# Column norms from squares, query weights turned by DMA, and a written order of decisions in a two-layer linear-attention kernel

## The chip, the cores and the metric

The kernel runs on one core of a Trainium2 chip. A core has a matrix engine (TensorE, PE in the profile), three engines for vectors (VectorE or DVE, ScalarE or ACT, GpSimd or POOL), an engine that issues transfers (SyncE, SP) and 16 DMA engines. Each engine works through its own list of instructions in order, and engines wait for each other on semaphores. The metric is the device time of one execution in microseconds, as a median over runs.

## The reference

There are 2048 tokens of 576 numbers, and two rounds of two blocks, each added to its input. Block A is linear attention with 32 heads of 18 numbers; its features are two softmaxes, of a small projection and of its negative. Block B multiplies two wide projections (4608 columns) and projects back. Both rounds use the same weights.

```python
qkv = (x @ wqkv) ...                       # q, k, v: 32 heads of 18
pq = einsum("bhsd,hdf->bhsf", q, w_phi)    # the same for pk from k
phi_q = concatenate([softmax(pq), softmax(-pq)])
kv = einsum("bhsf,bhsd->bhfd", phi_k, v);  z = sum of phi_k over tokens
o = (phi_q @ kv) / (phi_q . z + 1e-6);     A = o.reshape(B, S, D) @ wo
B = ((x @ w_gate) * (x @ w_up)) @ w_down
x = x + A(layernorm(x)); x = x + B(layernorm(x))     # twice
```

## The kernel before, in words

Tokens are cut into 16 tiles of 128 and, for block B, into 8 blocks of two tiles. The 576 channels are cut into four pieces of 128 and one of 64. The small matrix w_phi is folded into the query and key weights first: t_fuse1 (L1112) turns each of five 128-row pieces of the raw weights Wraw around (L1125, five matmuls with an identity into PSUM, and a copy at L1128 into WTk or WTq), multiplies by the block-diagonal BDphi (L1139) and evicts the two halves into Wk or Wq (L1144). A branch for turning them by DMA (L1120) is in the code and is not taken, since the string wtdma is empty.

Softmax needs no maximum when the logits are bounded. A flag decides this at run time. t_m2 (L971) finds the largest absolute entry of w_phi, and t_flag (L989) bounds the column norms of the query and key weights. For each of the five pieces it multiplies ten 128-column slices of Wraw by themselves into two PSUM banks (L999); the diagonals of these Gram matrices hold the squared norms, and a maximum over each row (L1002) is at least as large. A comparison (L1008), two matmuls with a vector of ones (L1010) that count the rows within the bound, and a last comparison (L1012) make the flag. Each engine then waits for the flag, loads it into a register and branches (emit_two, L221): one program without maxima ("fast") and one with them. What was recorded ahead of the flag is common to both; everything else lies behind the branch.

Stage one of layer 1 takes each tile through LayerNorm (t_ln, L1155; statistics L1179, normalised rows L1212, then turned by TensorE at L1223 for the first four tiles and by DMA at L1230 for the others), the V projection (t_v, L1463, eviction L1488) and the key projection (fast_front, L1363, exponentials L1377). softmax_tail (L1430) sums the features (L1444), inverts the sums, on DVE (L1447) or ACT (L1451, L1455), and multiplies (L1459, on POOL or DVE). Keys and values of a pair of tiles are then accumulated into two PSUM banks (L1498, t_ain). Query projections (t_qproj, L1387, copies at L1401 on ACT or L1402 on DVE) need nothing of that sum and can run at any time once Wq is there and the key tile given by pqg is done. After all 16 tiles t_barrier masks the sums, t_aout (L1598) forms the attention output of a tile, and block B starts on tiles 0 and 1 while later tiles follow in between: gate and up products (L1788), their product (L1835, L1837), and the down product (L1862, L1864). K, V and query projections run in pairs on the lower and upper 64 rows of the array (L1256, called row matmuls here); transposes, fusion and accumulation use the full array.

The order on every engine is fixed ahead of time by a planner in the kernel file (Sched, L316). Each piece of work is a thread that asks for an instruction or a group; the planner keeps an estimate of when each engine is free and takes the thread whose group could start first, moved forward or back by a priority, by an age from the code, and by an age from the table AGES (L19). Where a group is offered on two engines ("alt") it takes the one that ends first by its estimates. Engines keep the order in which their groups were taken. SP has one list as well: the loads of raw weights, tokens and V weights in the order of sload (L708), the transposing DMAs, the weights of block B.

## Time and profile before

| | |
|---|---|
| median of 5 runs | 1062.31 us |
| lowest and highest run | 1059.61 and 1062.66 us |
| profiled execution, its own time | 1061.52 us |
| its span, first to last instruction | 1059.7 us |
| mean granted TensorE clock | 0.998 |
| TensorE busy | 1052.1 us |
| VectorE, ScalarE, GpSimd busy | 480.3, 346.8, 190.7 us |
| DMA traffic | 127.78 MB |

A line of the timeline gives the start, the length, the engine, the line of the kernel, the operation, its output and inputs with their sizes, and in brackets how long the engine was idle before and what released it. In the answers by window the columns are the busy times of PE, PEld (the loading of matmul weights), DVE, ACT and POOL with their instruction counts, the granted clock, the DMA share and the traffic. Matmul ends are modelled, so the distance from one start to the next says what a matmul costs. A list of waits gives the total, the count and the longest.

### The profile page before, as it was taken

Reading aid. Unit: us, or ns where it says so; the run is one execution under the profiler, and the core shown is the slowest. Engines: PE = TensorE matmul, PEld = TensorE weight load, DVE = VectorE, ACT = ScalarE, POOL = GpSimd, SP = SyncE. Lnnn points to the kernel's source line nnn. Section 1 sums busy time; section 2 is a strip of 40 time slices with the busy share of each in tenths; the row PEclk is TensorE's granted clock in tenths of the full one; section 3 lists DMA queues with packets and bytes.
Section 4 is the critical chain, followed back from the end, with each engine's and each line's share of the span. In section 5 each row is a group of like instructions: output and inputs, shape, how many; then the busy total and the mean of one; then the engine's idle time right before and its main releaser. Section 6 shows DMA issues by size and latency. Waiting matters only on the chain.

```text
span 1059.7 us, 34388 instructions
## 1 busy us (share of the span) xinstructions
PE 1052.1 (99%) x15851; PEld 804.5 (76%) x15851; DVE 480.3 (45%) x972; ACT 346.8 (33%) x843; POOL 190.7 (18%) x204
## 2 busy tenths in 40 slices
PE   8999999999999999999999999999999999999998
PEld 6777868687786868778696786877778686868685
DVE  7865545264444536444232663534334343424131
ACT  6876224133241413225141742222313131202020
POOL 3962113030221203003110020201010101000000
PEclk9999999999999999999999999999999999999999
DMA  4595282552808165351616034545271918181704
GB/s 157 108 340 167 37 229 47 163 101 72 179 15 225 39 180 84 86 143 37 202 15 199 5 60 139 124 103 160 70 193 37 225 15 237 26 225 16 211 4 149
DMA packets 177625, 127.78 MB, mean 121 GB/s; under 512 B 96576, under 2 KB 175680, under 8 KB 176320
## 3 DMA queue, kind: packets, MB, share of 16 engines
q1 hardware_dynamic: 176864, 125.47, 45.5%
q8 instruction: 126, 2.06, 0.8%
q14 instruction: 27, 0.22, 0.1%
q10 hardware_dynamic: 608, 0.02, 0.0%
HBM read 100.82 MB, written 2.36 MB: 97 GB/s over the span
## 4 chain that ended last, share of the span: by engine, by line
PE 95%; DMA 2%; POOL 1%; ACT 1%; DVE 1%; issue 0%
PE ps L1788 54%; PE ps L1862 22%; PE ps L1256 12%; PE ps L1864 3%; PE ps L1646 1%; DMA wdr<-in_B_w_down_dram 1%; PE ps L1498 1%; PE ps L1244 0%; PE ps L1223 0%; POOL dd_w3f L1459 0%; POOL dd_h1g L1459 0%; DMA wdx<-in_B_w_down_dram 0%; ACT dd_h1g L1377 0%; DMA wst<-in_A_w_phi_dram 0%; POOL xln L1212 0%; PE ps L1139 0%
## 5 line engine op out<-in xcount | busy, mean ns | idle before, releaser
L1788 PE MATMUL ps<-xT,Wu 64*128 64x256 bf16 x4608 | 581.6, 269 | 0.0
L1788 PE MATMUL ps<-xT,Wg 64*128 64x256 bf16 x4608 | 581.1, 269 | 0.0
L1788 PEld LDWEIGHTS ps<-xT,Wg 64*128 64x128 bf16 x4608 | 431.2, 94 | 30.6 <-issue 3.3
L1788 PEld LDWEIGHTS ps<-xT,Wu 64*128 64x128 bf16 x4608 | 432.3, 94 | 27.6
L1837 DVE TENSOR_TENSOR hT<-ps,hT 128x512 bf16<-128x512 f32 x288 | 199.1, 691 | 302.5 <-ACT hT L1835 302.5
L1835 ACT CAST hT<-ps 128x512 bf16<-128x512 f32 x288 | 168.5, 585 | 400.5 <-PE ps L1788 396.2
L1862 PE MATMUL ps<-wdr,hT 128*128 128x512 bf16 x960 | 245.4, 380 | 0.4 <-DMA wdr<-in_B_w_down_dram 0.3
L1459 POOL TENSOR_TENSOR dd<-dd,ss 128x576 bf16<-128x576 bf16 x92 | 106.6, 1184 | 441.6 <-ACT ss L1455 441.6
L1864 PE MATMUL ps<-wdr,hT 128*128 128x64 bf16 x960 | 185.0, 193 | 0.0
L1862 PEld LDWEIGHTS ps<-wdr,hT 128*128 128x128 bf16 x960 | 93.7, 98 | 111.1 <-DMA wdr<-in_B_w_down_dram 1.8
L1788 PE MATMUL ps<-xT,Wr 64*128 64x256 bf16 x1152 | 165.5, 269 | 0.0
L1212 POOL TENSOR_SCALAR xln<-x_sb,nmean,rstd 128x576 bf16<-128x576 bf16 x56 | 45.5, 822 | 332.5 <-DVE nmean L1193 151.2
L1905 DVE TENSOR_TENSOR x_sb<-ps,x_sb 128x64 bf16<-128x64 f32 x32 | 7.0, 220 | 213.4 <-PE ps L1864 213.4
L1864 PEld LDWEIGHTS ps<-wdr,hT 128*128 128x128 bf16 x960 | 94.4, 98 | 0.2
L1455 ACT ACTIVATE ss<-ss 128x64 f32<-128x64 f32 x92 | 23.8, 259 | 195.9 <-DVE ss L1444 195.1
L1444 DVE TENSOR_REDUCE ss<-dd 128x64 f32<-128x1152 bf16 x48 | 63.7, 1345 | 16.6 <-ACT dd L1377 10.8
L1788 PEld LDWEIGHTS ps<-xT,Wr 64*128 64x128 bf16 x1152 | 63.2, 94 | 6.5
L1862 PE MATMUL ps<-wdx,hT 128*128 128x512 bf16 x192 | 54.4, 380 | 0.3 <-DMA wdx<-in_B_w_down_dram 0.3
L1256 PE MATMUL ps<-Wv,xT 64*128 64x288 bf16 x576 | 50.4, 288 | 0.2 <-ACT dd_h1g L1377 0.2
L1256 PE MATMUL ps<-Wk,xT 64*128 64x288 bf16 x576 | 48.4, 283 | 0.1
L1179 DVE BATCH_NORM_STATS2 st<-x_sb 128x6 f32<-128x288 bf16 x120 | 46.2, 445 | 0.8 <-DVE flag L1012 0.7
L1256 PE MATMUL ps<-Wq,xT 64*128 64x288 bf16 x576 | 40.6, 283 | 0.0
(131 smaller groups left out, 739.7 us busy)
## 6 DMA issues: line engine op xcount, KB each, us to landing
wdr<-in_B_w_down_dram SPq DMA_DIRECT2D x240, 288.0 KB, 3.6
wdx<-in_B_w_down_dram SPq DMA_DIRECT2D x48, 288.0 KB, 3.7
Wg<-in_B_w_gate_dram SPq DMA_DIRECT2D x4, 1152.0 KB, 17.1
Wu<-in_B_w_up_dram SPq DMA_DIRECT2D x4, 1152.0 KB, 18.5
out_dram<-x_sb SPq DMA_DIRECT2D x16, 144.0 KB, 2.5
x_sb<-in_A_x_dram SPq DMA_DIRECT2D x7, 288.0 KB, 3.2
Wraw<-in_A_wqkv_dram SPq DMA_DIRECT2D x5, 304.0 KB, 4.4
xT<-xln SPq DMA_TRANSPOSE x54, 2.5
```

Source lines behind the costliest of these rows:

```text
L1179: ops.append(Op(d_dve(288), (lambda e, j=j, h=h, src=src: e.bn_stats(st[:, sl[j], 6 * h:6 * h + 6], src)), reads=rd, writes=[("st", sl[j], ...
L1212: em = (lambda e, j=j: e.tensor_scalar(xln[:, sl[j], 0:576], x_sb[:, ss[j], :], s.nmean[:, sl[j]:sl[j] + 1], rstd[:, sl[j]:sl[j] + 1], ALU ...
L1256: out.append(Op(61, (lambda e, h=h, k=k, st=(i == 0 and k == 0), sp=(i == 1 and k == 3): e.matmul(s.ps[:, banks[h], 0:N], L[r, k, :], Wm[r ...
L1444: Op(1265, (lambda e: e.tensor_reduce(ss[:, sm, :], e4, AX.X, ALU.add)), reads=s.ddk(sm, 0) + s.ddk(sm, 1), writes=[("ss", sm)]),
L1455: yield ("ops", "act", [Op(200, (lambda e, kw=kw: e.activation(ss[:, sm, :], ss[:, sm, :], **kw)), reads=[("ss", sm)], writes=[("ss", sm)])])
L1459: yield ("alt", [(eng, [Op(dur, (lambda e, ev=ev, rb=rb: e.tensor_tensor(ev, ev, rb, ALU.mult)), reads=s.ddk(sm, br) + [("ss", sm)], write ...
L1498: ops.append(Op(d_pe(CW * n) + 3, (lambda e, k=k, c0=c0, h=h, n=n, st=(first and k == bi): e.matmul(s.ps[:, bank, c0:c0 + CW * n], phi[:, ...
L1788: out.append(Op(54.3, (lambda e, bank=bank, cs=cs, lhsT=lhsT, rhs=rhs, st=st, sp=sp: e.matmul(ps[:, bank, cs].rearrange("p (a n) -> p a n" ...
L1835: yield ("ops", "act", [Op(480, (lambda e, gb=gb, p=p: e.copy(hT[:, p, :], ps[:, gb, :])), reads=[("gu", gb)], writes=[("hT", p)] + (s.raw ...
L1837: yield ("ops", "dve", [Op(600, (lambda e, ub=ub, p=p: e.tensor_tensor(hT[:, p, :], ps[:, ub, :], hT[:, p, :], ALU.mult)), reads=[("gu", u ...
L1862: ops = [Op(d_pe(512), (lambda e: e.matmul(s.ps[:, bank, 0:512], lhsT, s.wslot(slot)[:, fi, 0:512], start=(f == 0), stop=(f == NF - 1))), ...
L1864: Op(d_pe(64) + 3, (lambda e: e.matmul(s.ps[:, z, 64 * sl:64 * sl + 64], lhsT, s.wslot(slot)[:, fi, 512:576], start=(f == 0 and (sl == 0 o ...
```

## The change

There are four edits. The flag's norms are no longer taken from Gram matrices: each piece of Wraw is squared (on ACT, or on POOL), nine matmuls per piece with a column of ones add the squares over rows into nine PSUM columns, and one maximum over nine columns follows; one comparison and one matmul take the place of two columns and two matmuls, and the limit is lowered by 1/64. The query weights are turned by the DMA branch of t_fuse1. Key and value accumulations are grouped by a list kvg, whose value gives the same pairs as before. And a text ORDER lists, decision by decision, which thread is to be taken next and in some places on which engine; as long as words are left, the planner takes the waiting thread whose next step stands first in the list, and an engine named there that is not on offer has no effect. The list ends in the second block of block B of layer 1; from there the old rule holds. Load order, ages and some settings are changed too: pqg is 10 in place of 4, and query copies are on ACT alone.

```diff
 AGES = {
...
 }
+ORDER = """
+init load side load side load load load load load/dve init load load init load/pool load init/pool load load init init init/dve lnA1_0b
+lnA1_0b/pool lnA1_0b m2 lnA1_0b m2 lnA1_0b m2/act lnA1_0b bdphi/pool fusek0/act fusek0 fusek1/dve fusek1 lnA1_0a sq0/dve m2/dve fusek0 sq0
+fusek1 lnA1_0a fusek0 fusek1 fusek4 sq2 fusek1/dve fusek4 sq1 fusek1 lnA1_0a/dve fusek2/act lnA1_0a fusek3 fusek2 fusek4/dve fusek2/act
+lnA1_0a fusek3/dve m2/dve lnA1_0a fusek4 fusek3 sq4 sq3 lnA1_0b fusek4 fusek0/pool lnA1_0a/dve lnA1_2/pool lnA1_2/act sq1 fusek3 lnA1_2/act
+fusek2/pool lnA1_1/pool fusek3 sq4 fusek0 sq2 sq3 v1_1 fusek4 lnA1_2 flag fusek3 fusek2 flag lnA1_2 fusek2 lnA1_2 lnA1_2/act lnA1_2 flag
+v1_1 v1_1/pool v1_1 flag fuseq0/pool ain1_0 lnA1_1 lnA1_2 lnA1_1 v1_0 lnA1_1 lnA1_2 lnA1_3 lnA1_3 ain1_0 v1_0/pool init lnA1_1 lnA1_1
...
+aout1_1 aout1_0 ain1_14 ain1_14 load ain1_15 ain1_15 ain1_15 pq1_2 ain1_15 v1_15 ain1_14 ain1_15 ain1_14 v1_15 v1_15 pq1_2/act load pq1_3
+ain1_15 pq1_2 pq1_4 pq1_2 pq1_3 pq1_5 pq1_3 pq1_4 aout1_0 aout1_1 pq1_3 pq1_6 pq1_4/act aout1_0 pq1_4 aout1_1/pool pq1_5/dve aout1_1
+ain1_15/dve aout1_0 aout1_0/pool pq1_6 pq1_5 ain1_15 ain1_15 pq1_5 pq1_7 aout1_0 ain1_15/act pq1_6 aout1_1 pq1_6 pq1_7/dve pq1_8/dve
...
+"""
...
+    def scripted(self):
+
+        best = None
+        for th in self.threads:
+            if th.req[0] in ("ops", "alt", "pe2", "dma"):
+                r_ = self.rank.get((th.name, self.steps.get(th.name, 0)))
+                if r_ is not None and (best is None or r_ < best[0]):
+                    best = (r_, th)
+        if best is None:
+            return None
+        th = best[1]
+        r = th.req
+        if r[0] == "alt":
+            pick = None
+            want = self.pick.get((th.name, self.steps.get(th.name, 0)))
+            for i_, (eng, ops) in enumerate(r[1]):
+                e_ = self.port_time(eng, ops[0], max(self.free_at[eng], self.ready(th, i_, eng, ops, False), th.t_ready))
+                f_ = (eng != want) * 1e9 * bool(want) + e_ + sum(o.dur for o in ops) * self.alt_cost[eng]
...
-            best = None
+            best = self.scripted() if self.left > 0 else None
+            told = best is not None
...
-        self.wtdma = ''
+        self.wtdma = 'q'
         self.valt = False
-        self.qalt = True
-        self.sload = [['raw', 2], ['raw', 1], ['x0', 0], ['raw', 0], ['raw', 3], ['x0', 1], ['x', 1], ['raw', 4], ['x', 2], ['wv', 0], ['x', 3]]
+        self.qalt = False
+        self.sload = [['x0', 1], ['raw', 1], ['raw', 0], ['x0', 0], ['raw', 2], ['raw', 4], ['x', 2], ['raw', 3], ['x', 3], ['wv', 0], ['x', 1]]
...
+        self.fqd = 1
+        self.kvg = [0, 2, 4, 6, 8, 10, 12, 14]
...
-        self.pqg = 4 if fast else 10
+        self.pqg = 10 if fast else 10
...
-        self.fqp = 6.15 if fast else 6.5
+        self.fqp = 6.5 if fast else 6.5
...
-        for kt in range(5):
-            yield ("wait", ("ld", "raw", rord[kt]))
-            if kt == 0:
-                gots = yield ("acqn", ["pb"], 2)
-                banks = [g_[1] for g_ in gots]
-            yield ("ops", "pe", [Op(55, (lambda e, m=m, c0=c0, kt=rord[kt], bank=banks[m // 3], c=128 * (m % 3), st=(kt == 0 and c0 == 0 and m in (0, 3)), sp=(kt == 4 and c0 > 0): e.matmul(
...
-        yield ("ops", "dve", [Op(d_dve(n), (lambda e, c=c, bank=bank, n=n: e.tensor_reduce(s.cst[:, c:c + 1], s.ps[:, bank, 0:n], AX.X, ALU.max)),
-                                 reads=[("pbd", bank)], writes=[("cst", c)], excl=[("pb", bank)]) for c, bank, n in ((1, banks[0], 384), (2, banks[1], 256))])
...
+        for i, kt in enumerate(rord):
+            if i < s.NSM:
+                sq, keys = s.dd[:, i].rearrange("p g b e -> p (g b e)"), s.ddk(i, 0) + s.ddk(i, 1)
+            else:
+                sq, keys = s.eT[:, 0].rearrange("p k n -> p (k n)"), [("eT", 0)]
+            yield ("go", s.t_square(i, kt, sq, keys), 9, "sq%d" % i)
...
+        for i in range(5):
+            yield ("wait", ("sq", i))
...
+        yield ("ops", "dve", [Op(130, (lambda e: e.tensor_reduce(s.cst[:, 1:2], s.ps[:, bank, 0:9], AX.X, ALU.max)), reads=[("pbd", bank)], writes=[("cst", 1)], excl=[("pb", bank)])])
...
+    def t_square(self, i, kt, sq, keys):
+        s = self
+        yield ("wait", ("ld", "raw", kt))
+        yield ("wait", "sqbank")
+        bank = s.sq_bank
+        W = s.Wraw[:, kt, 0:2 * D]
+        yield ("alt", [(eng, [Op(dur, em, reads=[("Wraw", kt)], writes=keys)]) for eng, dur, em in (
+            ("act", d_act(2 * D), lambda e: e.activation(sq, W, ACTF.Square)), ("pool", 2300, lambda e: e.tensor_tensor(sq, W, W, ALU.mult)))])
+        yield ("age", s.fage2)
+        yield ("ops", "pe", [Op(27, (lambda e, m=m: e.matmul(s.ps[:, bank, m:m + 1], sq[:, 128 * m:128 * m + 128], s.one16[:], start=s.sq_fresh(), stop=False, skip_group_check=True)),
+                                reads=keys + [("one16",)], writes=[("pbd", bank)], excl=[("pb", bank)]) for m in range(9)])
+        yield ("sig", ("sq", i))
```

## The prediction

> **What bounds the kernel now.** I read the page's first two parts, then short windows over the start, the timeline of the three engines around the flag, TensorE's own timeline up to the gate and up products, and last its waits.
>
> ```profile
> span 1059.7 us, 34388 instructions
> PE 1052.1 (99%) x15851; PEld 804.5 (76%) x15851; DVE 480.3 (45%) x972; ACT 346.8 (33%) x843; POOL 190.7 (18%) x204
> ```
>
> TensorE is busy for all but 7.6 us. The windows (columns: engine busy times, granted clock, DMA share, GB/s) show where the rest and the lost clock lie.
>
> ```profile
> 10.00:11.00 1.00, 1.00 (x22) 1.00 (x20) 0.96 (x3) 0.97 (x5) 0.00 (x0) 1.00 1.09 380
> 11.00:12.00 1.00, 0.39 (x9) 0.24 (x6) 0.96 (x3) 0.65 (x2) 0.82 (x1) 1.00 0.80 273
> 12.00:13.00 1.00, 0.16 (x2) 0.05 (x2) 0.36 (x2) 0.00 (x0) 0.00 (x0) 1.00 0.02 6
> 13.00:14.00 1.00, 0.91 (x14) 0.76 (x14) 0.93 (x3) 0.67 (x2) 0.82 (x4) 1.00 0.00 0
> 15.00:16.00 1.00, 1.00 (x11) 0.70 (x9) 0.68 (x4) 0.47 (x2) 0.00 (x0) 0.50 1.00 357
> ```
>
> TensorE stands almost still from 11.3 to 13.1 us, while the flag is made and the five engines branch on it; from 14.8 to 18.0 us its clock is 0.50 (0.81 in the microsecond from 14, 0.98 in that from 18). The first loads end at about 11.8 us: the share falls from 0.80 to 0.02. The timeline of that stretch:
>
> ```profile
> 10.43 0.89 DVE L1002 TENSOR_REDUCE cst<-ps 128x1 f32<-128x384 f32 x2
> 11.07 0.82 POOL L1212 TENSOR_SCALAR xln<-x_sb,nmean,rstd 128x576 bf16<-128x576 bf16 x1 [7.16 <-DVE cst L1002]
> 11.35 0.57 DVE L1008 TENSOR_SCALAR f<-cst 128x2 bf16<-128x2 f32 x1
> 11.97 0.19 PE L1010 MATMUL ps<-one,f 128*1 128x1 bf16 x2 [0.61 <-DVE f L1008]
> 12.22 0.14 DVE L1012 TENSOR_SCALAR flag<-ps 1x1 int32<-1x1 f32 x1
> 13.09 0.57 PE L1223 MATMUL ps<-ident,xln 128*128 128x128 bf16 x6 [0.93 <-DVE flag L1012]
> ```
>
> From the flag's start to TensorE's next matmul are 0.87 us. After 13.09 us TensorE is the bound nearly everywhere: its listed waits from there to 130 us are two of 0.2 us, and the down product waits 0.6 us for weights later. So this kernel's time is the moment of restart, plus TensorE's work behind it, plus what the clock takes. But one other engine is close:
>
> ```profile
> 30.00:40.00 10.00, 10.00 (x162) 7.58 (x164) 8.94 (x19) 8.59 (x32) 10.00 (x11) 1.00 0.85 146
> 40.00:50.00 10.00, 9.77 (x155) 7.01 (x151) 9.42 (x21) 7.55 (x28) 10.00 (x10) 1.00 0.23 52
> 50.00:60.00 10.00, 9.99 (x159) 7.36 (x157) 5.28 (x5) 9.17 (x32) 9.96 (x10) 1.00 0.93 165
> PE ps L1498 <- POOL dd_h1g L1459: 0.2, 1, 0.2
> ```
>
> The fifth busy time is POOL's: 29.96 of 30 us, and at 47.7 us TensorE does wait for it.
>
> **Query transposes to the DMA (A).** Removed are five groups of five L1125 matmuls for WTq and five copies out of PSUM. Start to next start on TensorE's timeline the groups take 0.39 (at 13.73), 0.38, 0.39, 0.37 and 0.38 us, together 1.9, all behind the restart where TensorE is full: -1.9. The copies (four on DVE at 0.48, one on ACT at 0.67) were 2.6 us beside other work. Added are five transposing DMAs of 128x640, the form of xT<-xln, whose median is 2.5 us to landing. They go on SP; in the written order the first is SP's first step after the branch, with the xT transposes of tiles 4 and 5 behind it. SP issues a pair of such transposes in 2.63 us, so these come up to 1.3 us late; TensorE has V and K projections of tiles 0 to 3 first. The other four are issued between loads and transposes on a queue with gaps (nothing between 13.9 and 24.8 us). Free as long as weights are ahead of their use; the last query weights were ready at 48 us and first used at 59.1. Without that cover a group of matmuls waits 2.5 us.
>
> **Norms from squares (G).** Fifty L999 matmuls go (a group of ten takes 0.47 to 0.67 us on the chain), with two L1002 reductions (0.89) and one of two L1010 matmuls. In come 45 matmuls of one column. Their price is between 25 and 36 ns: L1864's 64 columns start 30 ns before the next matmul, and five L1498 matmuls of 76 columns, each with weights of its own, start within 0.18 us. At 36 ns that is 1.6 us against 2.8 (0.056 x 50): 1.2 us of TensorE work less, but ahead of the restart, where TensorE waits for loads anyway; I count nothing for it. Also in: five squares of 128x1152, on ACT or POOL as the planner finds them free (the order's "dve" for the first is no choice on offer). ACT needs 0.69 for 640 columns and 0.40 for 288, about 0.8 ns a column, so 1.1 us; POOL 1.18 for 576, so 2.3 us. ACT is idle from 2.9 to 6.0 us and POOL from 3.9 to 11.1: three or four squares fit there; the one of the last weight load does not. One reduction of nine columns costs between L985's 0.13 and L982's 0.27.
>
> **What moves ahead of the branch (B).** In the order all 30 steps of the key fusion, both first LayerNorm tiles and the V projection of tile 1 stand before the fourth flag step. In the trace these follow the restart: L1223 x6 (0.35), L1139 x3 (0.29), L1139 x6 (0.79 at half clock, 0.28 at 0.14 for three), and 18 row matmuls at 0.0615 = 1.1. Together -2.0 at full clock.
>
> **The restart itself (D).** The first group of the V projection stands ahead of the flag matmul on TensorE, which is in order, and needs Wv. Wv is the tenth load with the same bytes before it as now, so it lands near the end of the first loads, 11.8 us. From there: ten row matmuls 0.62, three L1139 with a change of mode 0.24, the flag matmul 0.19, the wait and flag 0.2, then 0.73 from flag to matmul: 13.8. I take 13.9, +0.8. Below, the restart stays at 13.1 (Wv's large part issued at 5.07 with a median of 6.1 us to landing is there at 11.2). Above, all evictions come first. DVE's own work ahead of the flag is then 6.7 us (ten L1179 at 0.40, sums and signs 1.3, weight maximum and flag 1.4), ACT's 5.6 (three squares, Ln and Exp 1.5, two V evictions 0.8), and evictions on either are 8.2 (five WTk at 0.58, ten Wk at 0.41, two xT at 0.59): 20.5 us for two engines that begin at about 3.0 and 3.8 us, packed without a gap until 13.7; with 0.9 for two evictions that can't be packed and the 1.1 from flag matmul to restart 15.7, +2.6. I lean to the low end, because squares can use POOL.
>
> The small L1008 took 0.57 us and ended 0.03 us after POOL's L1212, while L1012 took 0.14. [...]
>
> **Clock (C).** Half clock for 3.2 us lost 1.6. After, TensorE has V matmuls beside the flag, but still some 0.9 us of branch and waits for loads. Either it falls again (0) or not (-1.6): I take -0.8, as the trace has one case and no other. [...]
>
> **Order of the K/V stage (E, F).** A full-array group between row groups costs two changes of about 0.105 us (row matmuls end at 21.13, transposes start 21.23, end 21.50, row matmuls start 21.61). From the restart to the last K/V accumulation I count 18 such blocks in the timeline and some 12 in the order; two of the six are in A: four times 0.2 is 0.8, and I take half, -0.4 (ends 0 and -0.8). New waits: TensorE will be three to four microseconds ahead of now, POOL has no reserve, but it starts earlier too (its first softmax multiply was at 23.6, TensorE's first K projection at 18.2 moves to about 14). Between 0 and the 6.2 of the rival below I take 1.0: nearest to the 0.6 idle that the trace shows there.
>
> Sum: -1.9 - 2.0 + 0.8 - 0.8 - 0.4 + 1.0 = -3.3 us. The profiled execution took 1061.5 (span 1059.7, 1.8 around it), 0.8 below the median of five runs; from the median, 1062.3 - 3.3 = 1059.0.
>
> **Rivals.** First, all covers hold: restart 13.1, no half clock, no new wait, -1.9 - 2.0 - 1.6 - 0.8 = -6.3, 1056.0. For it: three of five runs lie above 1062 and one at 1059.6, a spread of the size of the half clock. Against: the last square and Wv.
>
> Second, the softmax engines keep their pace and the saved TensorE time becomes waiting, so the gate and up products start at 93.5 as now: 1062.3. For it: POOL's 29.96 of 30 us. Against: they start three to four microseconds earlier as well, and DVE loses four copies.
>
> Third, slower: the query projections leave the K/V stage. Before, 100 of their matmuls (6.2 us) ran from 59.1 to 74.2 between the last K/V tiles; in the new order the first stands behind the first K group of tile 15, and their copies may use ACT alone. If softmax sets the pace there, TensorE idles for those 6.2 us and, as at 14.8 us, loses 1.6 to the clock: -4.3 + 6.2 + 1.6 = +3.5, 1065.8. It decides from 4.3 us of new idle on. Against: seven of these projections still precede the last accumulation.
>
> A late gate and up load is no rival: the last was issued at 61.7 and took at most 24.3 us, so it is there at 86.0, four microseconds ahead of the forecast start.
>
> **How the numbers follow.** The forecast's case 0.40, all covers 0.18, no gain 0.22, query projections 0.15, and 0.05 that the work ahead of the branch delays it by five microseconds or more. Two microseconds, 0.2%, is about what a measurement of this kernel can tell from no change: faster 0.58, same 0.22, slower 0.20. The range 1055.0 to 1065.0 leaves out the longer half of the slower cases and the shorter half of the first rival's, 0.1 each; the forecast's own is 1057.3 to 1060.6.
>
> **What would show it.** No L999 and no L1125 from Wq; restart between 13.1 and 15.7; no L1139 for the keys behind it; the first L1788 at about 90.2 instead of 93.5 and the rest of the trace as long as before. I am wrong if TensorE lists waits of several microseconds between 50 and 75 us, or the restart is past 16.

## The result, and the profile after

The changed kernel takes 1.0022 times the time of before (95% interval 1.0016 to 1.0029): 2.3 us slower, where 3.3 us faster was forecast. The medians were 1063.21 us (27 runs) and 1060.62 us (47 runs of before beside all comparisons). Its profiled execution took 1062.98 us, 1.5 more than that of before, and its page gives as span and busy times:

```profile
span 1061.2 us, 34348 instructions
PE 1049.6 (99%) x15832; PEld 804.7 (76%) x15832; DVE 478.5 (45%) x962; ACT 347.9 (33%) x842; POOL 198.7 (19%) x208
```

The work on TensorE is indeed less, 1049.6 us for 1052.1. What it stands idle went from 7.6 us to 11.6. The timeline of the engines up to the restart shows a first part of that:

```profile
5.64 1.39 POOL L1079 TENSOR_TENSOR BDphi<-wst,mask 128x720 bf16<-128x720 bf16 x1 [1.73 <-DMA wst<-in_A_w_phi_dram]
5.76 1.44 DVE L1346 TENSOR_SCALAR xln<-x_sb,nmean,rstd 128x576 bf16<-128x576 bf16 x1
6.99 4.24 POOL L1140 TENSOR_TENSOR dd<-Wraw 128x1152 bf16<-128x1152 bf16 x2
9.17 0.87 ACT L1278 CAST Wk<-ps 128x288 bf16<-128x288 f32 x2 [3.40 <-PE ps L1142]
13.16 1.53 DVE L1313 BATCH_NORM_STATS2 st<-x_sb 128x6 f32<-128x288 bf16 x4
14.85 0.77 DVE L1313 BATCH_NORM_STATS2 st<-x_sb 128x6 f32<-128x288 bf16 x2
15.53 0.15 DVE L1118 TENSOR_REDUCE cst<-ps 128x1 f32<-128x9 f32 x1
16.03 0.16 PE L1126 MATMUL ps<-one,f 128*1 128x1 bf16 x1
16.23 0.15 DVE L1128 TENSOR_SCALAR flag<-ps 1x1 int32<-1x1 f32 x1 [0.30 <-PE ps L1126]
17.11 0.42 PE L1390 MATMUL ps<-Wk,xT 64*128 64x288 bf16 x4 [0.32 <-issue]
```

L1140 are the squares, L1118 the maximum over nine columns, L1126 the flag's matmul, L1278 the copies of the fused key weights. TensorE restarts at 17.11 us; the forecast took 13.9. Two things are to be seen. Neither ScalarE nor VectorE is packed: ScalarE stands idle for 3.40 us until 9.17. And the statistics of three later LayerNorm tiles (13.16 and 14.85) stand on VectorE ahead of the maximum.

The windows that answer to those shown of before, and the waits of TensorE that the K/V stage and the first down product list:

```profile
30.00:40.00 10.00, 9.48 (x157) 6.92 (x154) 7.59 (x15) 7.87 (x29) 9.63 (x10) 1.00 0.80 115
40.00:50.00 10.00, 9.30 (x141) 6.38 (x143) 8.82 (x18) 7.27 (x25) 9.94 (x12) 1.00 0.34 74
50.00:60.00 10.00, 10.00 (x158) 8.25 (x155) 6.55 (x10) 8.31 (x29) 8.91 (x9) 1.00 0.94 164
...
PE ps L1632 <- POOL dd_h1g L1593: 0.6, 1, 0.6
PE ps L1632 <- DVE dd_h1g L1593: 0.5, 1, 0.5
PE ps L1273 <- DMA WTq<-Wraw: 0.4, 1, 0.4
PE ps L1390 <- ACT dd_h1g L1511: 0.3, 1, 0.3
...
PE ps L2000 <- DMA wdr<-in_B_w_down_dram: 1.2, 1, 1.2
```

From 30 to 50 us TensorE is busy for 18.78 us, where before it was 19.77. Between 20 and 90 us its idle time is 2.74 us instead of 0.62. It waits a little for each engine and once for a DMA that turns query weights.

The first gate and up product starts at 94.37 us (93.51 before), against 90.2 in the forecast. Behind it the trace is 0.64 us longer, with waits for down weights of 1.5 us instead of 0.6. So in these two executions the changed kernel gains nothing up to the gate, although by the count of the prediction (A and B) TensorE has some 4 us less to do behind the restart.

### The profile page after: what moved, and what is told of

Read it like the earlier page. It is cut to its first block, busy times and chain, and to the rows that moved or that the text cites. A ratio compares the mean times of both kernels' runs of the same rounds, so it can differ in the third digit from the quotient of the medians.

```text
span 1061.2 us, 34348 instructions
## 1 busy us (share of the span) xinstructions
PE 1049.6 (99%) x15832; PEld 804.7 (76%) x15832; DVE 478.5 (45%) x962; ACT 347.9 (33%) x842; POOL 198.7 (19%) x208
## 4 chain that ended last, share of the span: by engine, by line
PE 94%; DMA 2%; DVE 2%; ACT 1%; issue 0%; DVEq 0%; SPq 0%; ACTq 0%
PE ps L1926 53%; PE ps L2000 23%; PE ps L1390 11%; PE ps L2002 3%; PE ps L1784 1%; DMA wdx<-in_B_w_down_dram 1%; PE ps L1632 1%; ACT dd_h1g L1511 1%; PE ps L1378 1%; DMA WTq<-Wraw 1%; DVE dd_h1g L1593 0%; DMA wst<-in_A_w_phi_dram 0%; DVE ss_w4f L1578 0%; PE ps L1357 0%; DVE st L1313 0%; PE ps L1273 0%
## 5 line engine op out<-in xcount | busy, mean ns | idle before, releaser
L1346 POOL TENSOR_SCALAR xln<-x_sb,nmean,rstd 128x576 bf16<-128x576 bf16 x57 | 46.4, 823 | 321.7 <-DVE nmean L1327 148.3
L1390 PE MATMUL ps<-Wo,oT 64*128 64x288 bf16 x504 | 40.0, 283 | 0.0
```

The source lines that it names most:

```text
L1346: em = (lambda e, j=j: e.tensor_scalar(xln[:, sl[j], 0:576], x_sb[:, ss[j], :], s.nmean[:, sl[j]:sl[j] + 1], rstd[:, sl[j]:sl[j] + 1], ALU ...
L1390: out.append(Op(61, (lambda e, h=h, k=k, st=(i == 0 and k == 0), sp=(i == 1 and k == 3): e.matmul(s.ps[:, banks[h], 0:N], L[r, k, :], Wm[r ...
```

## The experiments

"Gate" below is the start of the first gate and up product, "restart" that of TensorE's first matmul behind the branch, both in the one profiled execution. Ratios are to the kernel before, with 95% intervals; 0.001 is 1.06 us.

**The start of the changed kernel.** In the first experiment eight steps of lnA1_2 and the first of lnA1_1 (statistics of tiles 2, 4 and 5 of the profile above) move in ORDER from ahead of the third and fourth flag step to behind the fourth. In the second the product BDphi goes from POOL to VectorE. The third has both.

```diff
- ... lnA1_2/pool lnA1_2/act sq1 fusek3 lnA1_2/act fusek2/pool lnA1_1/pool ... flag lnA1_2 fusek2 lnA1_2 lnA1_2/act lnA1_2 flag
+ ... sq1 fusek3 fusek2/pool ... flag fusek2 flag v1_1 v1_1/pool v1_1 flag lnA1_2/pool lnA1_2/act lnA1_2/act lnA1_1/pool lnA1_2 ...
```
```diff
- ... bdphi/pool fusek0/act
+ ... bdphi/dve fusek0/act
```

> The changed kernel with one edit of the written order: the statistics and row steps of tiles 2 to 5 (nine words) stand behind the flag instead of ahead of it. Theory 1 (the loss is made ahead of the branch, and VectorE's statistics in front of the flag's maximum are a part of it): the maximum over nine columns, now at 15.53 us though its matmuls are done at 14.4, comes about 1.1 us earlier; restart at about 15.9 in place of 17.1, first gate product at 93.3 in place of 94.4, time 1.1 us below the changed kernel, ratio to before about 1.0011. Theory 2 (the stage of K and V projections is paced by the softmax engines, whatever the restart): restart earlier, first gate product still at 94.4 within 0.3, ratio 1.002.

> The changed kernel with the block-diagonal product BDphi on VectorE instead of GpSimd. Theory 1 (the first LayerNorm row step took 1.44 us because GpSimd's BDphi ran beside it from 5.64 to 7.03): that row step takes 0.4 to 0.5 us, TensorE's first row transposes start near 6.3 instead of 7.25, restart 0.5 to 1.0 us earlier (16.3), ratio to before about 1.0015. Rival (the row step is slow for another reason, or the later steps hide it): it stays above 1 us, or the restart stays at 17.1; ratio 1.002.

> Both edits together: statistics behind the flag, and BDphi on VectorE. Theory 1: they add up; restart at about 15.2, first gate product at about 92.6, ratio to before 1.0003. Theory 2 (softmax engines set the pace up to the gate product): first gate product at 94 and ratio 1.002.

Statistics late: restart 16.02 instead of 17.11, but gate 97.33 and ratio 1.0052 (1.0039 to 1.0065). The longest new wait:

```profile
PE ps L1357 <- POOL xln L1346: 2.8, 1, 2.8
```

The statistics are cheap where they stood; taken back behind the flag they come into the stretch in which VectorE, ScalarE and POOL all have to feed TensorE, and one normalised tile is 2.8 us late. Behind that wait the granted clock reads 0.59 as a mean from 22 to 26 us, another 1.6 us. A restart 1.1 us earlier was worth less than that.

BDphi on VectorE: restart 19.55, gate 97.30, 1.0054 (1.0041 to 1.0067). The timeline of POOL and VectorE at its start (start, length, engine, ...):

```profile
4.58 2.11 POOL L1140 TENSOR_TENSOR dd<-Wraw 128x1152 bf16<-128x1152 bf16 x1 [0.66 <-DMA Wraw<-in_A_wqkv_dram]
4.85 2.00 DVE L1346 TENSOR_SCALAR xln<-x_sb,nmean,rstd 128x576 bf16<-128x576 bf16 x1
7.21 2.60 DVE L1079 TENSOR_TENSOR BDphi<-wst,mask 128x720 bf16<-128x720 bf16 x1
```

With POOL free earlier, a square starts there at 4.58, and the L1346 beside it needs 2.00 us instead of 0.42 alone; BDphi, 0.90 us on VectorE in the trace of before, needs 2.60 beside the next square. Taking POOL's first product away therefore lengthened work on VectorE at the start. It is not shown that this makes the whole of the later restart: in this profile TensorE also ran at half rate until about 13 us (ten transposes 1.17 us from start to start, 0.66 in the changed kernel), and its granted clock is 0.50 from 17 to 20 us. Both edits together: 1.0068 (1.0056 to 1.008), gate 99.26.

**One part of the change undone in its own order.** The query weights are turned by TensorE again (ORDER extended by the copies' words), the Gram matrices are back in place of the squares, or ORDER is empty.

```diff
-        self.wtdma = 'q'
+        self.wtdma = ''
```
```diff
-            yield ("go", s.t_square(i, kt, sq, keys), 9, "sq%d" % i)
...
+            yield ("ops", "pe", [Op(55, (lambda e, m=m, c0=c0, kt=rord[kt], bank=banks[m // 3], ...
```
```diff
-ORDER = """ init load side load ... """
+ORDER = ""
```

> The changed kernel with the query weights turned by TensorE again, everything else as changed: five groups of five matmuls more on TensorE and five copies more. If the DMA saves what was forecast, this is 1.5 to 1.9 us slower than the changed kernel, ratio to before about 1.004. If the transposing DMAs bring waits that eat the saving (one wait of 0.4 us for WTq is in the trace), it is the same or faster, ratio 1.002 or less.

> The changed kernel with the flag from Gram matmuls again: their groups of ten stand in the written order where the nine one-column matmuls stood, the squares are gone, the rest is as changed. If the squares cause the late restart: restart 1.5 to 2.5 us earlier than 17.1, and ratio to before 1.000. If the work put ahead of the flag causes it: restart at 16.5 or later, ratio 1.002.

> The changed kernel with an empty list of decisions: squares, DMA transposes, load order and ages as changed, the order by the planner's old rule. If the written order is what loses: restart at 15 or earlier and ratio 1.000 or below. If the squares and the load order lose: restart later than 15.5 and ratio 1.002 or above.

Transposes on TensorE: 1.0091 (1.0076 to 1.0105), gate 101.38, in ratio 7.3 us behind the changed kernel. That is far more than their 1.9 us of matmuls: idle time between 20 and 90 us is 5.63 us instead of 2.74, and two waits carry it:

```profile
PE ps L1390 <- ACT dd_h1g L1511: 1.7, 4, 0.7
PE ps L1273 <- DVE WTq L1262: 1.6, 3, 0.7
```

The copies out of PSUM, which the prediction put "beside other work", come between the eviction steps that TensorE waits for. Gram matrices: 1.0053 (1.0035 to 1.0071), restart 19.98, gate 97.36. No order: 1.0031 (1.002 to 1.0043), gate 98.53 with a granted clock of 0.50 from about 12.5 to 22.5 us. In the new order, then, the DMA is worth 7.3 us and the squares 3.3; the 1.0 of the order itself is not shown, since its interval meets that of the change. That says that the parts were fitted to each other; it doesn't say what each does to the kernel before.

**One part alone in the kernel before, planned anew.**

```diff
-        self.wtdma = ''
+        self.wtdma = 'q'
```
```diff
-            yield ("ops", "pe", [Op(55, (lambda e, m=m, c0=c0, kt=rord[kt], bank=banks[m // 3], ...
...
+            yield ("go", s.t_square(i, kt, sq, keys), 9, "sq%d" % i)
```

> The kernel before with one edit: the query weights are turned by DMA (the planner then plans anew by its old rule). If the forecast's first term holds by itself: five groups of matmuls and copies fewer behind the restart, 1.5 to 1.9 us faster, ratio 0.9984. Rival (the five DMAs come late on SP's list or the saved time turns into waits for the softmax engines): ratio 1.000 or above.

> The kernel before with the flag from squares and one-column matmuls, nothing else (planned anew by the old rule). If squares themselves delay the flag (1.15 us each on ScalarE or about 2.1 on GpSimd, the last behind the last weight load, and ScalarE's evictions behind them): restart at 14.5 to 16 in place of 13.1, ratio 1.001 to 1.003. If only the written order delays it: restart at 13.1 within 0.5, ratio 1.000.

Both are some 20 us slower: 1.0204 (1.0189 to 1.0218), gate 115.04, and 1.019 (1.0177 to 1.0203), gate 110.12. These runs price the planner and not the edit. In the first it issues the gate weights at 75 to 81 us, where before they were issued at 52 to 62. They tell nothing of A or G, and another way was needed.

**One part alone, everything else held.** The planner's decisions in the kernel before were written down as word lists, one for each side of the branch, and the changed kernel's own reading of such a list was put into the kernel before. Its instruction lists are then the same as before, and differ only by the edit. In the first the query weights come by DMA: the first DMA stands right behind the flag, the other four behind the loads of x, and the steps of matmul and copy are gone. In the second three squares go to ScalarE and two to POOL, with their matmuls where Gram matmuls stood. The third has both.

```diff
+ORDER_FAST = """
...
+"""
...
+        self.sc.script((ORDER_FAST if fast else ORDER_GENERAL).split())
...
-        self.wtdma = ''
+        self.wtdma = 'q'
...
-            if which == "q":
+            if which == "q" and not s.fast:
...
+            if kt > 0:
+                yield ("wait", ("w", which, kt - 1))
```
```diff
- ... load+7*2 flag+6*8 load load m2 load bdphi/dve m2 load fusek1 m2 load flag ...
+ ... load+7*2 sq0/act sq1/act load+6*8 load m2 load bdphi/dve m2 load fusek1 m2 load sq0 ...
```

> The kernel before with its whole plan (every decision, engine and warming matmul of both programs) written down and held, and one thing changed: the query weights are turned by five transposing DMAs right behind the branch. TensorE's list loses the five groups of five transposes and is otherwise the same; DVE loses four copies, ACT one. Theory 1 (the forecast's term A is right, and what the earlier run with DMA transposes in the kernel before lost was the new plan): first gate product at 91.6 instead of 93.5, ratio 0.9982 (-1.9 us). Theory 2 (the softmax engines or the weights keep the pace and the saving becomes waiting): 93.5, ratio 1.000. Theory 3 (the DMA transposes by themselves hold up the tiles' own DMA transposes or the loads): 95 or later, ratio above 1.002.

> The kernel before with its plan held, and only the Gram matrices replaced by squares (three on ACT, two on POOL, their matmuls where the Gram groups stood, the last two groups just before the last key fusion). Theory 1 (squares by themselves are worth about nothing; the late restart of the earlier run with squares in the kernel before, 17.3 us, came from the new plan): restart 13.0 to 13.9, time -0.3 to +0.8 us, ratio 0.9997 to 1.0008. Theory 2 (squares themselves delay the flag, since the last one stands behind the copies on ACT or takes 2.1 us on POOL): restart 15 or later, ratio 1.002 to 1.004.

> Both edits of the two runs above in the kernel before with its plan held; the written order of the change is left out. Theory 1: the two add up, -1.9 and -0.3 to +0.8, so -2.2 to -1.1 us, ratio 0.9979 to 0.9990, and the loss of the changed kernel lies in its order. Theory 2: no better than before, 1.000 or above, and the loss lies in the edits themselves.

DMA: 1.0013 (1.0001 to 1.0024), gate 94.09, restart 13.18. Squares: 1.0023 (1.0013 to 1.0033), gate 94.98, restart 14.88. Both: 1.0028 (1.0017 to 1.0039), gate 95.19. So with everything else in its place the DMA, forecast at -1.9 us, is +1.4 (0.1 to 2.5), the squares, forecast at 0, are +2.4 (1.4 to 3.5), and both are +3.0 (1.8 to 4.1). Against executions of before with the same mean granted clock, the DMA's sign stays: +0.9 us at 1.000 (3 executions against 13) and +1.5 at 0.998 (9 against 10). The change as a whole, +2.3 (1.7 to 3.1), lies 0.6 below that of both; the intervals overlap, so that the written order gives anything back isn't shown.

Where the 1.9 us of A went is seen on TensorE's timeline at a second query group. Before:

```profile
27.66 0.77 PE L1256 MATMUL ps<-Wv,xT 64*128 64x288 bf16 x8
28.36 0.45 PE L1125 MATMUL ps<-ident,Wraw 128*128 128x128 bf16 x5
28.75 0.79 PE L1256 MATMUL ps<-Wk,xT 64*128 64x288 bf16 x10
```

With the DMA (L1691 are the same row matmuls, L1812 the exponentials; L1574 is the fusion):

```profile
28.45 0.77 PE L1691 MATMUL ps<-Wv,xT 64*128 64x288 bf16 x8
28.94 0.28 PE L1691 MATMUL ps<-Wk,xT 64*128 64x288 bf16 x1
29.54 0.78 PE L1691 MATMUL ps<-Wk,xT 64*128 64x288 bf16 x9 [0.31 <-ACT dd_h1g L1812]
...
PE ps L1574 <- DMA WTq<-Wraw: 0.5, 1, 0.5
```

Before, V matmuls, five transposes and K matmuls follow each other without a listed wait. Without the transposes the first K matmul is early and the next nine wait until ScalarE's exponentials have freed a PSUM bank: from the start of the eight V matmuls to that of the long K group it is 1.09 us in both. There are three such waits, 0.7 us, one more of 0.3 for ScalarE, and 0.5 us at 15 us for the first turned weights; idle time from 20 to 90 us is 1.48 us instead of 0.62. At this place the transposes were work that stood in a gap: five matmuls less between two evictions don't make the evictions faster. The added idle time, 0.9 from 20 to 90 us and 0.5 ahead of it, is 1.4 us; the gate is 0.6 later although 1.9 of work went, so about 1 us of the loss is not located.

Where the squares lose is seen in TensorE's rate at the start. Ten transposes and the first fusion behind them, before and then with squares (L1585 and L1599 there; the first line of the second view is TensorE's first work, matmuls on zeros):

```profile
9.06 0.73 PE L1125 MATMUL ps<-ident,Wraw 128*128 128x128 bf16 x10
9.63 0.31 PE L1139 MATMUL ps<-BDphi,WTk 128*128 128x144 bf16 x3
```

```profile
1.04 2.64 PE L1395 MATMUL ps<-zt 128*128 128x128 bf16 x23 [1.04 <-DVE eps L1338]
9.98 1.25 PE L1585 MATMUL ps<-ident,Wraw 128*128 128x128 bf16 x10
11.02 0.48 PE L1599 MATMUL ps<-BDphi,WTk 128*128 128x144 bf16 x3
```

Ten transposes take 1.04 us from start to start instead of 0.57, and half rate lasts until about 18.5 us (ten V matmuls 16.58 to 17.89, 1.31 for 0.72). It is not a fall. All these profiles begin at half rate: the 23 matmuls on zeros start 0.105 us apart (sixteen of them from 1.04 to 2.72), where at full rate a 128x128 matmul takes 0.057. What differs is when half rate ends. With the Gram matmuls it had ended by 6 us in seven of eight profiles with the start of before (ten Gram matmuls 0.72 us long from 5.81 in the first of them); with squares it lasted to 18.5 us in both held runs. TensorE is busy for 6.83 of the nine microseconds from 1 to 10 without Gram matmuls, for 8.45 with them.

The eighth profile, that of the kernel before with POOL's multiplies halved (below), shows what half rate alone does. Ten Gram matmuls before, then there, and its restart:

```profile
5.81 0.72 PE L999 MATMUL ps<-Wraw 128*128 128x128 bf16 x10
```

```profile
6.36 1.27 PE L1434 MATMUL ps<-Wraw 128*128 128x128 bf16 x10
15.03 0.57 PE L1658 MATMUL ps<-ident,xln 128*128 128x128 bf16 x6 [0.93 <-DVE flag L1447]
```

No load is waited for in it, half rate lasts until 9.4 us, the restart is 1.9 us later than in the first profile and the gate at 95.77. So half rate at the start is enough, without squares, for a delay of the size that the squares bring (1.8 us). That it is the whole of their 2.4 us isn't shown: the rate of the other executions is not on record. Nor are Gram matmuls a guarantee, since in that profile they were there and TensorE was as busy.

**The changed kernel's order held, statistics back.** As in the first experiment, but with the changed kernel's plan held, so that TensorE's list stays as it is: only the statistics, ScalarE's and POOL's rows of tiles 4 and 5 move behind the flag and behind those of tiles 2 and 3.

```diff
- ... fusek0/pool lnA1_0a/dve lnA1_2/pool lnA1_2/act sq1 ...
+ ... fusek0/pool lnA1_0a/dve sq1 ... flag ... lnA1_1 ... lnA1_2/pool lnA1_2/act ...
```

> The changed kernel with its whole plan held (TensorE's list is the same, instruction by instruction) and the LayerNorm statistics of tiles 4 and 5 moved behind the flag; unlike the earlier run, tiles 2 and 3 keep their place ahead of them on DVE, ACT and POOL. Theory 1 (the statistics on DVE hold up the flag by 1.1 us, and the earlier run gave that back because the rows of tiles 2 and 3 came late): restart 16.0 instead of 17.1, no wait above 0.6 us for the rows, first gate product at 93.3, ratio to the kernel before 1.0012. Theory 2 (tiles 4 and 5 are then late, or the softmax engines keep the pace): first gate product at 94.4 or later, ratio 1.0022 or above.

1.0062 (1.0044 to 1.0079), restart 15.87, gate 96.72. TensorE waits 1.8 us for POOL in the accumulation and 1.1 for transposed tiles. The first experiment's answer holds without a new plan: the flag is 1.2 us earlier and the kernel 4 us slower.

**Is POOL the pace?** POOL was busy for 29.96 of 30 us, and the second rival built on it. Its softmax multiplies of layer 1's keys get half the heads, which leaves out half of that normalisation, in the kernel with the DMA and in the one before.

```diff
-            yield ("alt", [(eng, [Op(dur, (lambda e, ev=ev, rb=rb: e.tensor_tensor(ev, ev, rb, ALU.mult)),
+            g = 16 if s.fast and sm >= s.NSM else H
+            yield ("alt", [(eng, [Op(dur, (lambda e, ev=ev, rb=rb, g=g if eng == "pool" else H: e.tensor_tensor(ev[:, 0:g], ev[:, 0:g], rb[:, 0:g], ALU.mult)),
```

> The run with DMA transposes in the held plan of before, and POOL's softmax multiplies of the keys of layer 1 work on 16 of 32 heads (half of the normalisation is left out; nothing else changes). Theory P (POOL's chain sets the pace of the K/V stage, so the saved TensorE time became waiting): with POOL relieved TensorE's saving shows, its waits for the ACT logits' buffers after 26 us go, and the first gate product comes 1 to 2 us earlier than without the halving, at 92.0 to 93.0. Theory E (TensorE itself is the limit and the DMA transposes only cost): the same 94.1, within 0.3.

> The held plan of before with the same halving of POOL's multiplies and nothing else. Theory P1 (POOL alone sets the pace): first gate product 1 us or more earlier than 93.5. Theory P2 (TensorE and POOL are both full, either would do): 93.3 to 93.6, since TensorE has the same work and waited only 0.4 us in this stage; then a saving on TensorE alone is worth nothing and one on POOL alone is worth nothing.

With the DMA 1.0017 (1.0003 to 1.0031), without 0.9998 (0.9986 to 1.0011). POOL's busy time from 30 to 60 us falls to 19.6 and 20.3 us. That is worth nothing, and the waits of the kernel with the DMA stay: three of 0.7 us together for ScalarE's exponentials. POOL was full, and TensorE had waited for it for 0.2 us in the kernel before and for no listed time with the DMA. My theory that its chain sets the pace fell.

**Is it the clock?** Nine warming matmuls stand ahead of the flag's matmul, in the kernel before and in the kernel with the DMA (there with the first query fusion behind the 18 V matmuls, so that it does not wait).

```diff
- ... fusek2/act fusek2 flag fusek4/dve flag lnA1_0b ...
+ ... fusek2/act fusek2 flag+7*9 fusek4/dve flag lnA1_0b ...
```

> The held plan of before with nine warming matmuls (128x128, on zeros) ahead of the flag's matmul, where TensorE waits 0.6 us for the flag's comparison. Theory: TensorE is then idle for about 1 us instead of 1.8 and its clock does not fall, so the stretch from 14.8 to 18 us runs at full speed, keys come 1.2 to 1.6 us earlier, POOL's chain starts earlier too, and the first gate product comes 1.0 to 1.6 us earlier: ratio 0.9985 to 0.9990. Rival: the clock falls all the same, or POOL's chain starts where it did: 1.000.

> The held plan of before with the nine warming matmuls and the DMA transposes, and the first query fusion on TensorE moved behind 18 V matmuls so that it does not wait for its transpose (0.5 us in the run without). Theory P (POOL's chain sets the pace): POOL's second pair of rows starts 1.5 to 2 us earlier than in before (24.8 to 25.3 instead of 26.8), because TensorE reaches the keys earlier, and the first gate product comes 66.8 us behind it, at 91.6 to 92.1: ratio 0.9980 to 0.9987. If TensorE's saving counts in full: 93.5 - 1.6 - 1.9 = 90.0, ratio 0.9967. If neither: 93.5, 1.000.

1.0006 (0.9993 to 1.0018) and 1.0008 (0.9997 to 1.0019). In neither profile does the clock fall, and the gate is at 92.38 and 92.90; but waits for down weights are 2.0 and 3.4 us instead of 0.6, and neither ratio is clear of 1. With the DMA there is again no gain over its own base.

**The kernel before once more, and warmed earlier.** The same instructions as before, and a last version with eight warming matmuls on the bank that comes free first, so that they don't wait for an eviction.

```diff
- ... fusek2 flag fusek4/dve flag ...
+ ... fusek2 flag+99*8 fusek4/dve flag ...
...
+            b = b if b in self.pools["pb"]["free"] else min(self.pools["pb"]["free"], key=self.bank_time)
```

> The kernel before, unchanged, against itself. Expected: ratio 1.000 within 0.0012; first gate product at 93.5 within 0.3 (the plan up to there waits for little that varies). Theory N (the waits for down weights behind it differ between executions of the same program): these waits are not the 0.6 us of the first profile, but anything from 0.3 to 2, and the end of TensorE's work differs from the first profile by that. Theory K (they belong to the kernel): 0.5 to 0.7 us again, at the same two places.

> The held plan of before with eight warming matmuls ahead of the flag's matmul on a PSUM bank that is free one eviction earlier, so that they should not delay it (in the run with nine they ended 0.5 us after the comparison). Expected: restart at 13.1 to 13.3, no half clock, first gate product 1.3 to 1.6 us earlier than in before, at 91.9 to 92.2. If the gain up to the gate is kept: ratio 0.9985 to 0.9990 and a kernel faster than both; if the down weights then take it back: 1.000.

0.9999 (0.9985 to 1.0012) and 0.9999 (0.9988 to 1.0011). The repeat is the instructive one. Its gate is at 92.59, 0.92 us before that of the first profile of the same program; the V matmuls that ran at half clock there run at full clock here. The first profile, then the repeat:

```profile
14.12 0.93 PE L1256 MATMUL ps<-Wv,xT 64*128 64x288 bf16 x10
14.98 0.86 PE L1139 MATMUL ps<-BDphi,WTk 128*128 128x108 bf16 x6
16.16 2.18 PE L1256 MATMUL ps<-Wv,xT 64*128 64x288 bf16 x18
```

```profile
14.61 0.79 PE L1256 MATMUL ps<-Wv,xT 64*128 64x288 bf16 x10
15.33 0.58 PE L1139 MATMUL ps<-BDphi,WTk 128*128 128x108 bf16 x6
16.08 1.27 PE L1256 MATMUL ps<-Wv,xT 64*128 64x288 bf16 x18
```

Ten V matmuls take 0.72 us, 0.86 in the first profile, eighteen 1.12 us instead of 2.01, and the granted clock is not 0.50 anywhere before TensorE's last matmul. Yet the execution took 1063.7 us, 2.2 more than the first: it waits 1.5 us for one kind of down weights alone. In the last one a load of raw weights was late (TensorE waits 1.60 us for it at 8.47, though it was there by 6.77 before), the restart was 14.79, and the time was 1062.3. So the half clock comes in some executions of this program and not in others, and a gate 1 us earlier or later in a single profile is no verdict. No version here is clearly faster than the kernel before.

How often it comes can be read from the mean granted clock that is on record for each execution. The 1.6 us of the first profile lower a mean over 1060 us by 0.0015. Of 106 executions of the kernel before that ran beside the experiments, 53 have a mean of 1.000 and take 1061.0 us on average; 44 have 0.998 or 0.997 and take 1062.7; nine lie between. The difference, 1.7 us, has the same sign in all five groups of runs (0.9 to 2.4). With warming matmuls 32 of 34 executions have 0.999 or more, and still they are no faster than before as a whole: if the clock gives something back, it is lost elsewhere, and where isn't shown. In the lists the clock has no place in time, so that a late wait brought both the fall and the longer time isn't excluded for single executions.

## Why the prediction was wrong, step by step

**A, "all behind the restart where TensorE is full: -1.9": this step failed, and with it the sign.** The matmuls went as counted; their time did not. Held in place the step measured +1.4 (0.1 to 2.5); between the kernels with POOL halved it is +2.0 and between the two warmed ones +0.2, with intervals of more than 1 us on either: no gain in any of three comparisons. Being busy for 99% of the span was taken as proof that TensorE is the bound. Where its timeline was compared, it was busy because transposes stood where it would have waited for ScalarE to free a bank. What was late next, and not named in the sum, were the exponentials (1.0 us in four waits) and the first turned weights (0.5). The prediction's price for a missed DMA was 2.5 us and its verdict "free as long as weights are ahead"; the first was not ahead, by 0.5.

The busy share did not show it: that of the matmuls is 99% before and after, that of the weight loads 76% in both, and 1.9 us of matmuls taken out brought nothing.

**G, "I count nothing for it": failed by 2.4 us.** The price of one matmul was right: nine start to the next group within 0.23 to 0.26 us, 26 to 29 ns each, inside the bounds of 25 to 36. The squares were right too: 1.15 to 1.17 us on ScalarE (1.1 taken), 2.1 on POOL (2.3 taken). What was put at nothing without a reason was TensorE's rate: work ahead of the restart was called free because TensorE "waits for loads anyway", while in the held kernel it stayed at half rate to 18.5 us and the restart came 1.8 us later. In the changed kernel's own profile the rate is full by 7.25 us (ten transposes from 7.76 to 8.42 us); there 38 matmuls on zeros in place of 23 keep TensorE busy until 5.28. That these make the difference wasn't tried, and the run with BDphi on VectorE has the same 38 and half rate until 13 us. What the squares cost in the changed kernel's profile is therefore a part of D.

**D, the restart: taken 13.9, upper end 15.7, measured 17.11.** It exceeds even the bound that the text set for being wrong. The evictions had been called "packed without a gap". In fact VectorE is busy for 10.75 and ScalarE for 8.02 of the 13.4 us from 3.0 to 16.4: 18.8 us, less than the 20.5 counted, and 8.0 us of gaps beside them. Fusions wait for evictions there (TensorE 0.30 us for ScalarE's at 10.10 us, 0.20 for VectorE's at 11.43) and evictions for fusions; that this chain makes all of the gaps is argued. The statistics ahead of the maximum are 1.1 us of the delay (first experiment). The upper end was therefore no bound: it summed two engines' work and left out the chain between them and TensorE.

**B, E, and the balance.** The work of B stands ahead of the branch in the trace, as counted; E was not measured by itself. By the two profiles: gate +0.86 = +4.0 from the restart, +2.1 from more idle time between 20 and 90 us (F), -1.6 because the clock did not fall (C), and the rest, -3.6, for A, B and E together, taken at -4.3. The forecast for the gate was -3.3, so of the 4.2 us missed D has 3.2, F 1.1 and the rest 0.7, while C gave back 0.8. The -3.6 is a remainder and no measurement, and A's own run shows no saving: in the changed kernel the restart is the largest step that failed, and in the kernel before A and G fail by themselves.

**C, -0.8: right for the two profiles that it compared, not for the average.** The half clock appears in four of five unwarmed profiles with the start of before (the first one, and three with its start held) and not in the repeat of the same program; with warming matmuls it appears in none of three. By the record of single executions (above) it comes in about half of those of the kernel before, and costs about what C took. But in the changed kernel too only 13 of 29 executions have a mean clock of 1.000 (1062.5 us on average; the others 1064.0), as against 53 of 106 before. So the falls are as frequent as they were, and their saving in the one profile is luck.

**F, +1.0 of new waits: 2.1 measured**, inside its ends of 0 and 6.2. It is spread over POOL, VectorE, ScalarE and a DMA, so no single one is the cause.

**The rivals.** The second, that saved TensorE time becomes waiting, was right in kind. Its engine was wrong for the kernel before with the DMA, where TensorE waits for ScalarE's banks and half of POOL's work is worth nothing; in the changed kernel TensorE does wait for POOL, 0.6 us, and for VectorE, 0.5. The small chance of 0.05 on work ahead of the branch delaying it came true at 4.0 us, not quite the five it was given. The third did not happen: there is no wait of several microseconds between 50 and 75 us. The time itself, 1063.2, is inside the range of 1055 to 1065. The chances were not: 0.20 for slower was too little, because each of the three rivals was worked out as a single event, while what came was a late restart and small waits together.

What stays open: whether the written order gives back part of the 3.0 us, whether half rate makes the whole 2.4 us of the squares, where about 1 us of the DMA's loss lies, and what decides when half rate ends at the start.

## What to carry to other kernels

An engine that is busy for 99% isn't shown to be the bound: look at what its instructions between two waits are, since filler that is taken out can turn into the wait that it covered. Before removing work that seems to cost nothing or to be pure gain, ask what it kept going (a rate, a bank's turn), and price an edit of a planned kernel with the plan held, as planning anew around it cost 20 us here where the edit was worth 2. And profile the same program twice before reading 1 us from one profile, and sort executions by their granted clock before comparing means.

## What the hardware showed that I had not expected

- The same instructions had a clock of 0.50 for some 3 us in one execution and none in another (eighteen V matmuls 2.01 us from start to start and 1.12). The two profiles of the kernel before differ at the start too: the first ten Gram matmuls have 1.01 us in one and 1.25 in the other.
- With the Gram matmuls gone and the plan held, TensorE ran at half rate from its first matmul to about 18.5 us (ten transposes 1.04 us for 0.57) while the granted clock in the windows reads 1.00 throughout. The start-to-start times decide; the clock column alone would have hidden it.
- At that half rate nine one-column matmuls still took 0.24 to 0.26 us in four of five groups, as at full rate (0.23 to 0.26), while transposes took 1.8 times as long.
- A bf16 tensor_scalar of 128x576 on VectorE takes 0.42 us alone, 1.44 beside BDphi on POOL and 2.00 beside a POOL square of 2.11 us. The prediction had noted a small case (L1008 with 0.57 us, ending 0.03 us after a LayerNorm row on POOL); that a tensor_tensor on VectorE goes from 0.90 to 2.60 beside such a square it had not.
- The start differs from one execution to the next: of eight profiles with the start of before (three of them with warming matmuls in it) the restart is at 13.09 to 13.62 us in six, at 14.79 in one in which a load was 1.6 us late, and at 15.03 in one in which half rate lasted to 9.4 us.
